# Pinned scans and logarithms, a new order at the end of the first tile's attention, and leaky factors on GpSimd

## The chip, the cores and the metric

One core of a Trainium2 chip runs the whole program. The metric is the device time of one execution in microseconds (us); less is better. The engines are named TensorE (PE, with its weight loads PEld), VectorE (DVE), ScalarE (ACT), GpSimd (POOL) and SyncE (SP, which issues most DMAs). Each engine has a queue of its own and does its instructions in the order in which they stand there; semaphores make one engine wait for another.

## What is computed

A gated linear attention over 4 batches, 8 heads, 768 tokens and head size 48, then a layer with a leaky activation whose slope alpha is given per column, then a gated layer. Cut to what matters:

```
for t in range(S):                       # q, k, v, alpha: (4, 8, 768, 48)
    state = alpha[:, :, t, :, None] * state + einsum('bhd,bhe->bhde', k[:, :, t], v[:, :, t])
    y[:, :, t] = einsum('bhd,bhde->bhe', q[:, :, t], state)
x = y.transpose(0, 2, 1, 3).reshape(B * S, H * D)          # 3072 x 384
h = x @ w_in                                               # 384 x 2048
x = (maximum(h, 0) + moe_alpha * minimum(h, 0)) @ w_out    # 2048 x 384
out = (((x @ w1) * (x @ w2)) @ w3) @ w_out2                # 384 x 1024, 1024 x 1024, 1024 x 384
```

The weights come as 64-bit words and are put together on the chip. Results have to keep float32 accuracy, so each factor of a large product is kept as an upper and a lower half (hi, lo), and three matmuls (hi by hi, lo by hi, hi by lo) take the place of one.

## The kernel before

**Attention.** The recurrence is done in 24 chunks of 128 tokens, n = 0 to 23, six to a batch. For each chunk `prep(n)` takes the running product of alpha over the chunk with a scan on VectorE (line 221, in place in one of two buffers, al), forms qt = q times that product (line 228), lets ScalarE take logarithm and exponential (r, lines 235 and 236) and forms kn from k and r in three VectorE steps (lines 237 to 239). GpSimd copies the last column (pend, line 232) and sets the first column of the buffer to zero (line 225). `scores(n)` multiplies qt and kn on TensorE (scp, line 244) and masks the result on VectorE (sc, line 279); `kT(n)` transposes kn (kTp, line 263; ScalarE copies it to kT). `chunk(n)` does the state matmuls (Up or uy), the update of the state on VectorE (`advance`: sst, lines 300 to 304), the output (`yout`: uy and yp) and then the scores of the next chunk. The outputs go by DMA into x, whose halves `xsplit` makes (hi on ScalarE, lo on VectorE, line 363).

**The two layers.** Four chunks make a tile T of 512 tokens, six tiles in all. A step (T, f) with f = 0 to 15 is `G1`, nine matmuls into h (line 407), and the activation: u on ScalarE (line 419), g on VectorE (line 421), gs hi on ScalarE (line 426), gs lo on VectorE (line 427); and `G2` two steps later, nine matmuls into three accumulator banks acc (lines 435 to 438). At f = 15 ScalarE copies the accumulators out (x1e), which frees their banks; uy, scp and kTp of the next tile's chunks use the banks of the same set. The factors sgn and salpha that u, g and gs take are computed from moe_alpha once, at the start. After tile 5 the gated layer follows from about 430 us on (ab, cs); the change does not touch it.

**What sets the order.** At the start a list of small functions, `first`, is run through: the attention of tile 0, with a few warm-up matmuls (wu) on zeros between them, so that TensorE is not idle. Then a sequence of steps mixes tile 0 with tile 1 (14 steps later) and goes through tiles 2 to 5 one after the other. After each `G1` and each `G2` the function `attend` runs some of the next tile's attention units, in the order that `attn_units` gives: chunk(n), kT(n + 1), prep(n + 2). In tile 0, and at every second step of tiles 2 to 4, a weight block is put together (`convert`: top on ScalarE, line 142; y on VectorE, line 149; for the first 16 blocks w hi on ScalarE and w lo on VectorE, line 154; the others go back to memory by DMA, line 182). The order of SyncE's DMAs is as written. On the other engines a scheduler may move an instruction ahead of ones written earlier where its inputs are ready; `keep_in_program_order` pins an instruction behind the one written before it on its engine. Before, pinned are u and g of tiles 2 to 5, the scan of chunk 4, and the y of some blocks.

Of the kernel before, what the change touches and what calls it, by code (L numbers as in the profile page):

```python
# [15 lines left out]
AF = mybir.ActivationFunctionType  # L16
AX = mybir.AxisListType
ALU = mybir.AluOpType
# [14 lines left out]
SPT = TA // CH  # L33
NTA = NT // TA
NF = DFF // 128
# [6 lines left out]
EARLY = 2  # L42
# [22 lines left out]
def fused_kernel(ctx, tc, qk, al, vv, wf, ws, m_alpha, ident, maskn, out):  # L65
# [3 lines left out]
    def f32(ap):  # L69
        return ap.bitcast(F32)  # L70

    def copy(out, in_):
        act.activation(out=out, in_=in_, func=AF.Copy)  # L73
# [93 lines left out]
    def convert(i, last=False):  # L167
        t = raw.pop(i)
        n = t.shape[1]
        if i == 0 or i >= NF:  # L170
            upper(top, t, i >= NF)
        y = cp.tile([128, n], I32, tag="y", name="y", bufs=1)
        ins = assemble(y, top, t)
        if last or i >= NF:
            tc.keep_in_program_order(ins)
        if i + 1 < NF:
            upper(top, raw[i + 1])
        if i < NF:
            split(wt[i][:, :, 0], wt[i][:, :, 1], f32(y).rearrange("p (o c) -> p o c", o=2), dve)
        else:  # L180
            c = (i - NF) * BLK
            later(1, lambda: sp.dma_start(out=ws_d[:, c:c + n], in_=f32(y)))
# [29 lines left out]
        v = st["v", n] = ap2.tile([128, H, DP], F32, tag="v", name="v", bufs=3)  # L212
        sp.dma_start(out=v, in_=vv[b, c])

    def prep(n, last=False):
        if n >= NSTEP:
            return
        t = st.pop(("qk", n))
        P = albuf[n % 2]
        flatP = P.rearrange("p a t -> p (a t)")  # L220
        scan = dve.tensor_tensor_scan(out=flatP, data0=flatP, data1=scan1.rearrange("p a t -> p (a t)"),  # L221
                                      initial=0.0, op0=ALU.mult, op1=ALU.max)
        if last:
            tc.keep_in_program_order(scan)
        pool.memset(P[:, :, 0:1], 0.0)
        Pv = P[:, :, 1:]
        qt = ap2.tile([128, NP, CH], F32, tag="qt", name="qt")
        dve.tensor_tensor(out=qt, in0=t[:, 0], in1=Pv, op=ALU.mult)
        r = ap2.tile([128, NP, CH], F32, tag="r", name="r", bufs=1)
        kn = ap2.tile([128, NP, CH], F32, tag="kn", name="kn")  # L230
        pend = ap2.tile([128, NP, 1], F32, tag="pend", name="pend")
        pool.tensor_copy(out=pend, in_=P[:, :, CH:])
        st["pend", n], st["qt", n], st["kn", n] = pend, qt, kn

        act.activation(out=r, in_=Pv, func=AF.Ln)
        act.activation(out=r, in_=r, func=AF.Exp, scale=-1.0)
        dve.tensor_tensor(out=kn, in0=t[:, 1], in1=r, op=ALU.mult)
        dve.tensor_tensor(out=r, in0=Pv, in1=r, op=ALU.mult)
        dve.scalar_tensor_tensor(out=kn, in0=r, scalar=2.0, in1=kn, op0=ALU.subtract, op1=ALU.mult)
# [44 lines left out]
    def state(n, w, ps):  # L284
        if ends(n):
            return
        t, v = st.pop(("kT", n)), st["v", n]
        for p, hh, r in pairs:
            mm(ps[r, p], t[:, p, r], v[:, 2 * p + hh], start=True, stop=True)

# [13 lines left out]
            dve.tensor_tensor(out=new, in0=new, in1=pend, op=ALU.mult)  # L304

    def yout(n, w, shared):
        qt, v = st.pop(("qt", n)), st.pop(("v", n))
        sc = [st.pop(("sc", n, hh)) for hh in range(2)]
        alone = n % NC_B == 0
        ps = [shared[:, 1] if n >= SPT else bank([128, NP // 2, CH], "yp", w), pab.tile([128, NP // 2, CH], F32, tag="h", name="yp")]  # L310
        half = [slice(64 * a, 64 * a + DP) for a in range(2)]
        for hh in range(2):
            for i in range(NP // 2):
                for a in range(2):
                    p = 2 * i + a
                    mm(ps[hh][half[a], i], v[:, 2 * p + hh], sc[hh][:, p], start=i == 0, stop=alone and i == NP // 2 - 1,
                       skip_group_check=True)
        if not alone:
            for i in range(NP // 2):
                for hh, a in ((0, 0), (1, 1), (0, 1), (1, 0)):  # L320
                    mm(ps[hh][half[a], i], sst[n % 2][half[hh], 2 * i + a], qt[half[hh], 2 * i + a], start=False,
                       stop=i == NP // 2 - 1, skip_group_check=True)
        T, c = divmod(n, SPT)
        if c == 0:
            new_x(T)
        single = n in (2, 3)
        if single:
            y = gp.tile([128, NP, CH], F32, tag="x1", name="yT1", bufs=KD)
            for hh in range(2):
                copy(y[:, 2 * hh:2 * hh + 2], ps[hh])  # L330
        else:
            if c % 2 == 0:
                st["yT"] = ap2.tile([128, KD, NP // 2, 2, CH], F32, tag="yT", name="yT", bufs=1)
            y = st["yT"]
            if n < SPT or ends(n):
                copy(y[:, 1, :, c % 2], ps[0])
            else:
                copy(y[:, :2, :, c % 2], shared)
                advance(n, y[:, 0, :, c % 2].rearrange("q i (a e) -> q i a e", a=2))
            copy(y[:, 2, :, c % 2], ps[1])  # L340
            if c % 2 == 0:
                return
            y = y[:, 1:].rearrange("p h i c t -> p (h i) (c t)")
        x = f32(xt[T][:, 1, :, (c if single else c - 1) * CH:(c + 1) * CH])

        def place():
            q = (sp, act) if n == SPT - 1 else (sp, sp)
            for hh in range(2):
                q[hh].dma_start(out=x[hh * D:(hh + 1) * D], in_=y[64 * hh:64 * hh + D, :KD])
            for i, (k, to, hh, e, n_) in enumerate(PIECES):  # L350
                q[i % 2].dma_start(out=x[to:to + n_, k], in_=y[64 * hh + e:64 * hh + e + n_, KD])

        later(1 if n < SPT or c == SPT - 1 else 4, place)
# [3 lines left out]
    def new_x(T):  # L357
        xt[T] = xp.tile([128, 2, KD, TA], F32R, tag="x", name="x")

    def xsplit(T, c, n):  # L360
        hi, lo = (xt[T][:, a, :, c * CH:(c + n) * CH] for a in range(2))
        copy(hi, f32(lo))
        dve.tensor_tensor(out=lo, in0=f32(lo), in1=f32(hi), op=ALU.subtract)

    def chunk(n, w, more=True):
        if n > 3:
            load_v(n + 2)
        untie()
        if n < SPT:
            ps = bank([128, NP, DP], "Up", w)  # L370
            state(n, w, ps)
            advance(n, ps)
            yout(n, w, None)
        else:
            ps = bank([128, 2, NP // 2, CH], "uy", w)
            state(n, w, ps[:, 0].rearrange("q i (a e) -> q (i a) e", a=2))
            yout(n, w, ps)
        if more:
            scores(n + 1, w)
        if n < 3:  # L380
            load_v(n + 3)
# [30 lines left out]
    def G1(T, f):  # L412
        x, w = xt[T], r_in[f]
        ps = pab.tile([128, TA], F32, tag="h", name="h")
        mm3(ps, [(w[:, i, k], x[:, 0, k]) for k in range(KD) for i in range(2)]
            + [(w[:, 0, k], x[:, 1, k]) for k in range(KD)], True, True)
        sg, sa = sgn[:, f:f + 1], salpha[:, f:f + 1]
        u = gp.tile([128, TA], F32, tag="m", name="u", bufs=1)
        both = [act.activation(out=u, in_=ps, func=AF.Identity, scale=sg)]  # L419
        gt = gp.tile([128, TA], F32, tag="g", name="g")  # L420
        both += [dve.scalar_tensor_tensor(out=gt, in0=ps, scalar=sa, in1=u, op0=ALU.mult, op1=ALU.max)]  # L421
        if T > 1:
            for ins in both:
                tc.keep_in_program_order(ins)
        s = g_t[T, f] = gp.tile([128, 2, TA], F32R, tag="gs", name="gs", bufs=3)
        act.activation(out=s[:, 0], in_=gt, func=AF.Identity, scale=sg)  # L426
        dve.scalar_tensor_tensor(out=s[:, 1], in0=gt, scalar=sg, in1=f32(s[:, 0]), op0=ALU.mult, op1=ALU.subtract)  # L427
# [17 lines left out]
    with tc.manual_schedule(engines={mybir.EngineType.SP}):  # L445
# [18 lines left out]
        def warm_up(n):  # L464
            ps = pab.tile([128, 512], F32, tag="h", name="wu")
            for _ in range(n):
# [6 lines left out]
        fetch(1)  # L473
        prep(1)
        load(3)
        dve.tensor_scalar(out=sgn, in0=alpha, scalar1=1.0, scalar2=-2.0, op0=ALU.is_gt, op1=ALU.mult)
        dve.tensor_scalar(out=sgn, in0=sgn, scalar1=1.0, scalar2=None, op0=ALU.add)
        dve.tensor_tensor(out=salpha, in0=alpha, in1=sgn, op=ALU.mult)
        first = [lambda: scores(0, 0), lambda: kT(0, 0), lambda: chunk(0, 0), lambda: (kT(1, 0), fetch(EARLY)), lambda: prep(2),
                 lambda: (load(4), chunk(1, 0)), lambda: kT(2, 0), lambda: prep(3),  # L480
                 lambda: chunk(2, 0), lambda: kT(3, 0), lambda: conv_next(True), lambda: xsplit(0, 0, 2),
                 lambda: chunk(3, 0, False), lambda: (warm_up(REST), conv_next(True), load(5)), lambda: (prep(4, True), load(6)),
                 lambda: xsplit(0, 2, 2)]
        for u in first:
            u()
            warm_up(WARM)
# [335 lines left out]
```

## Time and profile before

| | us |
|---|---|
| median of 3 runs | 847.43 |
| lowest, highest | 844.17, 847.84 |
| the profiled execution | 846.02 |
| its span in the trace | 844.2 |
| TensorE busy | 824.3 (98%) |
| VectorE busy | 458.3 (54%) |
| ScalarE busy | 355.3 (42%) |
| GpSimd busy | 10.3 (1%) |

The span runs from the first to the last instruction in the trace; what lies around it is 1.8 us. Busy shares are means over the whole span, and the start, the stretch with attention and the rest differ. The idle time that stands in brackets behind a row, with its releaser, is the time in which that engine had nothing to do ahead of that row.

### The profile page before, as it was taken

Reading aid. Unit: us, or ns where it says so; the run is one execution under the profiler, and the core shown is the slowest. Engines: PE = TensorE matmul, PEld = TensorE weight load, DVE = VectorE, ACT = ScalarE, POOL = GpSimd, SP = SyncE. Lnnn points to the kernel's source line nnn. Section 1 sums busy time; section 2 is a strip of 40 time slices with the busy share of each in tenths; the row PEclk is TensorE's granted clock in tenths of the full one; section 3 lists DMA queues with packets and bytes.
Section 4 is the critical chain, followed back from the end, with each engine's and each line's share of the span. In section 5 each row is a group of like instructions: output and inputs, shape, how many; then the busy total and the mean of one; then the engine's idle time right before and its main releaser. Section 6 shows DMA issues by size and latency. Waiting matters only on the chain.

```text
span 844.2 us, 12696 instructions
## 1 busy us (share of the span) xinstructions
PE 824.3 (98%) x5160; PEld 673.1 (80%) x5160; DVE 458.3 (54%) x643; ACT 355.3 (42%) x562; POOL 10.3 (1%) x53
## 2 busy tenths in 40 slices
PE   8989999999999999999999999999999999999996
PEld 4567888888887788878888889988888888888885
DVE  7799966774766576765345634652434425322221
ACT  4568764534544554554335634522223232222222
POOL 0000000000000000000000000000000000000000
PEclk9999999999999999999999999999999999999999
DMA  8647555330774377354104207320402203010101
GB/s 314 212 168 245 197 176 183 118 110 10 225 236 146 119 231 256 131 165 168 48 3 159 78 1 255 119 75 1 150 0 75 75 31 119 1 38 0 38 1 41
DMA packets 49106, 99.60 MB, mean 118 GB/s; under 512 B 4880, under 2 KB 25488, under 8 KB 49040
## 3 DMA queue, kind: packets, MB, share of 16 engines
q1 hardware_dynamic: 48800, 98.62, 34.6%
q8 instruction: 42, 0.69, 0.3%
q14 instruction: 24, 0.20, 0.1%
q10 hardware_dynamic: 240, 0.10, 0.0%
HBM read 75.63 MB, written 18.35 MB: 111 GB/s over the span
## 4 chain that ended last, share of the span: by engine, by line
PE 83%; DMA 2%; DVE 1%; ACT 1%; issue 0%; SPq 0%; DVEq 0%; ACTq 0%
PE ab L407 23%; PE h L407 20%; PE acc L407 12%; PE acc L435 6%; PE acc L438 6%; PE acc L436 6%; PE w L407 4%; PE uy L244 3%; DMA al<-in_al_dram 2%; PE scp L244 2%; PE yp L244 1%; PE kTp L263 1%; DVE al L221 0%; DVE y L149 0%; ACT u L419 0%
## 5 line engine op out<-in xcount | busy, mean ns | idle before, releaser
L407 PE MATMUL h<-x,w 128*128 128x512 f32 x864 | 214.3, 392 | 3.2 <-ACT w L73 1.4
L407 PE MATMUL ab<-x,w 128*128 128x512 f32 x864 | 203.6, 389 | 0.0
L407 PEld LDWEIGHTS h<-x,w 128*128 128x128 f32 x864 | 160.9, 188 | 39.8 <-DVE g L421 2.6
L407 PEld LDWEIGHTS ab<-x,w 128*128 128x128 f32 x864 | 162.1, 188 | 33.6
L435 PE MATMUL acc<-gs,w 128*128 128x512 f32 x288 | 114.7, 398 | 0.0
L614 DVE TENSOR_TENSOR c<-ab,a 128x512 f32<-128x512 f32 x48 | 33.1, 690 | 147.3 <-PE ab L407 147.3
L436 PE MATMUL acc<-gs,w 128*128 128x512 f32 x288 | 112.3, 390 | 0.0
L421 DVE SCALAR_TENSOR_TENSOR g<-h,salpha,u 128x512 f32<-128x512 f32 x96 | 71.8, 748 | 69.2 <-ACT u L419 69.1
L407 PE MATMUL acc<-cs,w 128*128 128x512 f32 x432 | 105.8, 389 | 0.0
L426 ACT ACTIVATE gs<-g,sgn 128x512 fp32r<-128x512 f32 x96 | 69.3, 722 | 75.5 <-DVE g L421 75.4
L419 ACT ACTIVATE u<-h,sgn 128x512 f32<-128x512 f32 x96 | 65.4, 681 | 82.5 <-PE h L407 82.4
L427 DVE SCALAR_TENSOR_TENSOR gs<-g,sgn,gs 128x512 fp32r<-128x512 f32 x96 | 71.9, 749 | 42.7 <-ACT gs L426 42.6
L407 PEld LDWEIGHTS acc<-cs,w 128*128 128x128 f32 x432 | 81.0, 188 | 17.2 <-DVE cs L617 0.4
L438 PE MATMUL acc<-gs,w 128*128 128x512 f32 x288 | 80.9, 389 | 0.0
L73 ACT ACTIVATE a<-ab 128x512 f32<-128x512 f32 x48 | 28.7, 597 | 111.9 <-PE ab L407 111.9
L73 ACT ACTIVATE cs<-c 128x512 fp32r<-128x512 f32 x48 | 30.2, 630 | 91.5 <-DVE c L614 91.5
L435 PEld LDWEIGHTS acc<-gs,w 128*128 128x128 f32 x288 | 54.1, 188 | 12.6 <-issue 1.2
L438 PEld LDWEIGHTS acc<-gs,w 128*128 128x128 f32 x288 | 54.1, 188 | 11.5
L436 PEld LDWEIGHTS acc<-gs,w 128*128 128x128 f32 x288 | 54.1, 188 | 10.5
L617 DVE TENSOR_TENSOR cs<-c,cs 128x512 fp32r<-128x512 f32 x48 | 33.2, 691 | 30.8 <-ACT cs L73 30.8
L142 ACT ACTIVATE top<-raw 128x768 f16<-128x768 bf16 (+1 forms) x39 | 41.8, 1071 | 16.9 <-DVE y L149 12.0
L221 DVE TENSOR_TENSOR_SCAN al<-al,scan 128x516 f32<-128x516 f32 x24 | 29.4, 1230 | 25.2 <-DMA al<-in_al_dram 25.2
(73 smaller groups left out, 673.8 us busy)
## 6 DMA issues: line engine op xcount, KB each, us to landing
raw<-in_ws_dram SPq DMA_DIRECT2D x22, 767.8 KB, 5.2
qk<-in_qk_dram SPq DMA_DIRECT2D x24, 512.0 KB, 5.9
raw<-in_wf_dram SPq DMA_DIRECT2D x16, 767.8 KB, 5.9
ws_d<-y SPq DMA_DIRECT2D x22, 384.0 KB, 2.6
al<-in_al_dram SPq DMA_DIRECT2D x24, 256.0 KB, 4.9
v<-in_vv_dram SPq DMA_DIRECT2D x24, 256.0 KB, 5.9
alx<-in_al_dram SPq DMA_DIRECT2D x8, 768.0 KB, 4.6
x_d<-x1e SPq DMA_DIRECT2D x18, 256.0 KB, 4.3
```

The costliest lines, as they stand in the source:

```text
L73: act.activation(out=out, in_=in_, func=AF.Copy)
L142: ins = act.activation(out=z[:, :n].bitcast(F16).rearrange("p (n c) -> p n c", c=2)[:, :, 1], in_=t.bitcast(BF16)[:, :, 2], func=AF.Copy)
L244: ins = pe.matmul(*a, **k)
L407: pe.matmul(ps, w, x, start=first and i == 0, stop=last and i == n - 1)
L419: both = [act.activation(out=u, in_=ps, func=AF.Identity, scale=sg)]
L421: both += [dve.scalar_tensor_tensor(out=gt, in0=ps, scalar=sa, in1=u, op0=ALU.mult, op1=ALU.max)]
L426: act.activation(out=s[:, 0], in_=gt, func=AF.Identity, scale=sg)
L427: dve.scalar_tensor_tensor(out=s[:, 1], in0=gt, scalar=sg, in1=f32(s[:, 0]), op0=ALU.mult, op1=ALU.subtract)
L435: pe.matmul(acc[T][m], r_out[f][:, 0, c], s[:, 0], start=f == 0, stop=False)
L436: pe.matmul(acc[T][m], r_out[f][:, 1, c], s[:, 0], start=False, stop=False)
L438: pe.matmul(acc[T][m], r_out[f][:, 0, c], s[:, 1], start=False, stop=f == NF - 1)
L617: dve.tensor_tensor(out=s[:, 1], in0=c, in1=f32(s[:, 0]), op=ALU.subtract)
```

## The change

It has six parts. (1) The scan and the logarithm of the preparations of chunks 9 to 23 are pinned behind the instruction written before them on their engine. (2) u and g are pinned from tile 1 on, where it was tile 2. (3) In `first`, the second weight conversion, load(5), the long warm-up and the second split of x are written inside prep(4), between its scan and its logarithm, instead of before and after prep(4); scan, logarithm and that split are pinned. (4) In chunk 3 the output is written ahead of the state matmuls and the update. (5) sgn and salpha are computed on GpSimd instead of VectorE; ahead of them the compiled program has one more row of GpSimd that loads a library. (6) The top half of weight block 2 is written at the conversion of block 2 itself, no more at that of block 1.

```
 def prep(n, last=False, between=None):
...
+        if last or n > 2 * SPT:
+            tc.keep_in_program_order(scan)
         if last:
-            tc.keep_in_program_order(scan)
+            between()
...
-        act.activation(out=r, in_=Pv, func=AF.Ln)
+        ln = act.activation(out=r, in_=Pv, func=AF.Ln)
+        if last or n > 2 * SPT:
+            tc.keep_in_program_order(ln)
         act.activation(out=r, in_=r, func=AF.Exp, scale=-1.0)
...
 def convert(i, last=False):
-        if i == 0 or i >= NF:
+        if i in (0, EARLY) or i >= NF:
             upper(top, t, i >= NF)
...
-        if i + 1 < NF:
+        if i + 1 < NF and i + 1 != EARLY:
             upper(top, raw[i + 1])
...
 def xsplit(T, c, n, last=False):
-        copy(hi, f32(lo))
-        dve.tensor_tensor(out=lo, in0=f32(lo), in1=f32(hi), op=ALU.subtract)
+        both = [act.activation(out=hi, in_=f32(lo), func=AF.Copy),
+                dve.tensor_tensor(out=lo, in0=f32(lo), in1=f32(hi), op=ALU.subtract)]
+        if last:
+            for ins in both:
+                tc.keep_in_program_order(ins)
...
 def chunk(n, w, more=True):
         if n < SPT:
+            if n == SPT - 1:
+                yout(n, w, None)
             ps = bank([128, NP, DP], "Up", w)
             state(n, w, ps)
             advance(n, ps)
-            yout(n, w, None)
+            if n < SPT - 1:
+                yout(n, w, None)
...
 def G1(T, f):
-        if T > 1:
+        if T > 0:
             for ins in both:
                 tc.keep_in_program_order(ins)
...
-        dve.tensor_scalar(out=sgn, in0=alpha, scalar1=1.0, scalar2=-2.0, op0=ALU.is_gt, op1=ALU.mult)
-        dve.tensor_scalar(out=sgn, in0=sgn, scalar1=1.0, scalar2=None, op0=ALU.add)
-        dve.tensor_tensor(out=salpha, in0=alpha, in1=sgn, op=ALU.mult)
+        pool.tensor_scalar(out=sgn, in0=alpha, scalar1=1.0, scalar2=-2.0, op0=ALU.is_gt, op1=ALU.mult)
+        pool.tensor_scalar(out=sgn, in0=sgn, scalar1=1.0, scalar2=None, op0=ALU.add)
+        pool.tensor_tensor(out=salpha, in0=alpha, in1=sgn, op=ALU.mult)
...
-                 lambda: chunk(3, 0, False), lambda: (warm_up(REST), conv_next(True), load(5)), lambda: (prep(4, True), load(6)),
-                 lambda: xsplit(0, 2, 2)]
+                 lambda: chunk(3, 0, False),
+                 lambda: prep(4, True, lambda: (conv_next(True), load(5), warm_up(REST), xsplit(0, 2, 2, True))),
+                 lambda: load(6)]
```

What the pins do to the order shows at three places. The first is VectorE in tiles 1 and 2, around the scan of chunk 14 (al_109 holds the even chunks, al_110 the odd ones). Before, it stands among the steps at the end of tile 1, right behind a kn of chunk 13:

```order
L279 TENSOR_TENSOR sc<-scp,msk 128x512 x2
L237 TENSOR_TENSOR kn<-qk,r 128x512
L221 SCALAR_TENSOR_TENSOR al_109<-al_109,scan_111 128x516
L238 TENSOR_TENSOR r<-al_110,r 128x512
L421 SCALAR_TENSOR_TENSOR g<-h,salpha,u 128x512
L239 SCALAR_TENSOR_TENSOR kn<-r,kn 128x512
```

After, it stands in tile 2, behind gs lo of that tile's third step, and qt, kn, r, kn follow it at once:

```order
L437 SCALAR_TENSOR_TENSOR gs<-g,sgn,gs 128x512
L431 SCALAR_TENSOR_TENSOR g<-h,salpha,u 128x512
L437 SCALAR_TENSOR_TENSOR gs<-g,sgn,gs 128x512
L221 SCALAR_TENSOR_TENSOR al_109<-al_109,scan_111 128x516
L230 TENSOR_TENSOR qt<-qk,al_109 128x512
L241 TENSOR_TENSOR kn<-qk,r 128x512
L242 TENSOR_TENSOR r<-al_109,r 128x512
L243 SCALAR_TENSOR_TENSOR kn<-r,kn 128x512
L306 TENSOR_TENSOR sst_112<-sst_113,yT 128x256
L149 SCALAR_TENSOR_TENSOR y<-raw,top 128x768
L431 SCALAR_TENSOR_TENSOR g<-h,salpha,u 128x512
```

So the scan went some ten steps back, from tile 1 to the last place ahead of its use. The second place is TensorE at that use, the scores of chunk 14, in the fourth step of tile 2. Before, they follow the output matmuls of chunk 13:

```order
L244 MATMUL uy<-qt,sst_113 64x128
L244 MATMUL yp<-qt,sst_113 64x128
L244 MATMUL scp<-qt,kn 64x128 x16
L435 MATMUL acc_2339<-gs,w_82 128x512
L436 MATMUL acc_2339<-gs,w_82 128x512
L435 MATMUL acc_2340<-gs,w_82 128x512
L436 MATMUL acc_2340<-gs,w_82 128x512
```

After, four accumulating matmuls of the next G2 have come ahead of them:

```order
L248 MATMUL uy<-qt,sst_113 64x128
L248 MATMUL yp<-qt,sst_113 64x128
L445 MATMUL acc_2336<-gs,w_82 128x512
L446 MATMUL acc_2336<-gs,w_82 128x512
L445 MATMUL acc_2337<-gs,w_82 128x512
L446 MATMUL acc_2337<-gs,w_82 128x512
L248 MATMUL scp<-qt,kn 64x128 x16
```

The third place is ScalarE at the end of tile 2, where the copies x1e free the accumulators. Before, the logarithm and the exponential of chunk 19 (the two rows r) stand between gs hi and these copies:

```order
L419 ACTIVATE u<-h,sgn 128x512
L426 ACTIVATE gs<-g,sgn 128x512
L235 ACTIVATE r<-al_110 128x512
L236 ACTIVATE r<-r 128x512
L73 ACTIVATE x1e<-acc_2339 128x512
L73 ACTIVATE x1e<-acc_2340 128x512
L73 ACTIVATE x1e<-acc_2341 128x512
```

After, the copies follow gs hi directly:

```order
L429 ACTIVATE u<-h,sgn 128x512
L436 ACTIVATE gs<-g,sgn 128x512
L73 ACTIVATE x1e<-acc_2336 128x512
L73 ACTIVATE x1e<-acc_2337 128x512
L73 ACTIVATE x1e<-acc_2338 128x512
L73 ACTIVATE yT<-uy 128x4x128
```

The two rows of chunk 19 now come five steps later, in tile 3.

## Rows read from the trace of the kernel before

**Rows 1.** The page, first part: TensorE (PE), its weight loads and the other engines, busy us, share of the span, count.

```profile
PE 824.3 (98%) x5160; PEld 673.1 (80%) x5160; DVE 458.3 (54%) x643; ACT 355.3 (42%) x562; POOL 10.3 (1%) x53
```

**Rows 2.** The table of two stretches: start and end, length, busy us of PE, PEld, DVE, ACT and POOL with their counts, granted clock, DMA share, GB/s.

```profile
50.00:60.00 10.00, 8.51 (x64) 6.26 (x62) 10.00 (x15) 6.23 (x10) 1.21 (x4) 1.00 0.71 248
400.00:700.00 300.00, 300.00 (x1394) 253.77 (x1393) 131.21 (x174) 106.90 (x175) 0.00 (x0) 1.00 0.24 78
```

**Rows 3.** The list of waits, those of TensorE: us in total, times, longest.

```profile
PE uy L244 <- ACT x1e L73: 2.4, 2, 1.4
PE Up L244 <- ACT kT L73: 1.9, 3, 1.2
PE scp L244 <- DVE kn L239: 1.7, 2, 1.4
PE h L407 <- ACT w L73: 1.4, 1, 1.4
```

**Rows 4.** The timeline at the end of tile 2 (start, length, engine, line, operation), and the scores of chunk 19.

```profile
285.79 1.23 DVE L221 TENSOR_TENSOR_SCAN al<-al,scan 128x516 f32<-128x516 f32 x1 [1.27 <-DMA al<-in_al_dram]
286.94 0.73 DVE L427 SCALAR_TENSOR_TENSOR gs<-g,sgn,gs 128x512 fp32r<-128x512 f32 x1
287.06 0.63 ACT L235 ACTIVATE r<-al 128x512 f32<-128x512 f32 x1 [1.78 <-DVE al L221]
...
287.72 0.63 ACT L236 ACTIVATE r<-r 128x512 f32<-128x512 f32 x1
288.25 1.55 ACT L73 ACTIVATE x1e<-acc 128x512 f32<-128x512 f32 x3
288.88 0.69 PE L244 MATMUL uy<-v,kT 128*64 128x64 f32 x16 [1.41 <-ACT x1e L73]
...
316.72 1.10 PE L244 MATMUL scp<-qt,kn 48*64 48x128 f32 x32
```

**Rows 5.** The timeline in tile 2 at 255 to 260 us.

```profile
255.76 1.23 DVE L221 TENSOR_TENSOR_SCAN al<-al,scan 128x516 f32<-128x516 f32 x1 [4.55 <-DMA al<-in_al_dram]
...
259.74 2.35 PE L407 MATMUL h<-x,w 128*128 128x512 f32 x9 [1.01 <-DVE g L421]
```

**Rows 6.** The timeline of one step of tile 2: h has ended at the first row, and the next h begins at the last.

```profile
278.70 0.39 PE L435 MATMUL acc<-gs,w 128*128 128x512 f32 x1
...
278.96 0.69 ACT L419 ACTIVATE u<-h,sgn 128x512 f32<-128x512 f32 x1 [0.88 <-PE h L407]
...
279.68 0.75 DVE L421 SCALAR_TENSOR_TENSOR g<-h,salpha,u 128x512 f32<-128x512 f32 x1 [0.61 <-ACT u L419]
...
280.47 0.72 ACT L426 ACTIVATE gs<-g,sgn 128x512 fp32r<-128x512 f32 x1 [0.82 <-DVE g L421]
...
280.74 2.20 PE L407 MATMUL h<-x,w 128*128 128x512 f32 x9
281.23 0.75 DVE L427 SCALAR_TENSOR_TENSOR gs<-g,sgn,gs 128x512 fp32r<-128x512 f32 x1 [0.79 <-ACT gs L426]
```

**Rows 7.** The timeline of a preparation that nothing else delays, that of chunk 0, from its exponential on; and one update of the state.

```profile
5.93 0.63 ACT L236 ACTIVATE r<-r 128x512 f32<-128x512 f32 x1
...
6.59 0.69 DVE L237 TENSOR_TENSOR kn<-qk,r 128x512 f32<-128x512 f32 x1 [0.39 <-ACT r L236]
7.32 0.69 DVE L238 TENSOR_TENSOR r<-al,r 128x512 f32<-128x512 f32 x1
8.04 0.69 DVE L239 SCALAR_TENSOR_TENSOR kn<-r,kn 128x512 f32<-128x512 f32 x1
...
261.74 0.42 DVE L302 TENSOR_TENSOR sst<-sst,yT 128x256 f32<-128x256 f32 x1
```

**Rows 8.** The timeline of TensorE at the end of the h ahead of the scores of chunk 14 and at these scores; between them the last kn of chunk 15, and behind them that chunk's scores.

```profile
213.84 0.39 PE L435 MATMUL acc<-gs,w 128*128 128x512 f32 x1
...
213.96 0.69 DVE L239 SCALAR_TENSOR_TENSOR kn<-r,kn 128x512 f32<-128x512 f32 x1
...
219.54 1.05 PE L244 MATMUL scp<-qt,kn 48*64 48x128 f32 x32
...
235.43 1.05 PE L244 MATMUL scp<-qt,kn 48*64 48x128 f32 x32
```

**Rows 9.** The timeline of TensorE in one chunk: the first state matmul and the scores.

```profile
253.43 0.69 PE L244 MATMUL uy<-v,kT 128*64 128x64 f32 x16
...
255.40 1.06 PE L244 MATMUL scp<-qt,kn 48*64 48x128 f32 x32
```

**Rows 10.** The timeline around 58 to 60 us: top of weight block 5, w hi of block 4 and the h that takes it.

```profile
58.20 1.07 ACT L142 ACTIVATE top<-raw 128x768 f16<-128x768 bf16 x1 [1.18 <-DMA raw<-in_wf_dram]
...
59.14 0.81 ACT L73 ACTIVATE w<-y 128x768 fp32r<-128x768 f32 x1
...
60.01 0.49 PE L407 MATMUL h<-x,w 128*128 128x512 f32 x1 [1.36 <-ACT w L73]
```

**Rows 11.** The timeline: the first of the three factor operations on VectorE, GpSimd's memset behind the scan of chunk 2, SyncE's load of chunk 4; and from the page's list of DMA issues (KB each, median us to landing) the loads of alpha.

```profile
14.58 0.17 DVE L476 TENSOR_SCALAR sgn<-alpha 128x16 f32<-128x16 f32 x1
16.43 0.10 POOL L225 MEMSET al<- 128x4 f32 x1 [6.26 <-DVE al L221]
19.55 0.55 SPq L204 DMA_DIRECT2D al<-in_al_dram  x1
al<-in_al_dram SPq DMA_DIRECT2D x24, 256.0 KB, 4.9
```

More of the change, by code (lines that the diff above doesn't have):

```diff
@@ L213, in load_v, with prep @@
         sp.dma_start(out=v, in_=vv[b, c])
-    def prep(n, last=False):
+    def prep(n, last=False, between=None):
         if n >= NSTEP:
@@ L286, in state @@
             return
-        t, v = st.pop(("kT", n)), st["v", n]
+        t, v = st.pop(("kT", n)), st.pop(("v", n)) if n == SPT - 1 else st["v", n]
         for p, hh, r in pairs:
@@ L306, in yout @@
     def yout(n, w, shared):
-        qt, v = st.pop(("qt", n)), st.pop(("v", n))
+        qt, v = st.pop(("qt", n)), st["v", n] if n == SPT - 1 else st.pop(("v", n))
         sc = [st.pop(("sc", n, hh)) for hh in range(2)]
@@ L358, in new_x, with xsplit @@
         xt[T] = xp.tile([128, 2, KD, TA], F32R, tag="x", name="x")
-    def xsplit(T, c, n):
+    def xsplit(T, c, n, last=False):
         hi, lo = (xt[T][:, a, :, c * CH:(c + n) * CH] for a in range(2))
-        copy(hi, f32(lo))
-        dve.tensor_tensor(out=lo, in0=f32(lo), in1=f32(hi), op=ALU.subtract)
+        both = [act.activation(out=hi, in_=f32(lo), func=AF.Copy),
[3 more added lines that the diff above has]
+                tc.keep_in_program_order(ins)
     def chunk(n, w, more=True):
```

## The prediction

> **What bounds the kernel now.** I read the page first: TensorE is busy for 824.3 us of a span of 844.2 [rows 1], so only what makes TensorE wait, or lets it wait less, can move the time. The profiled execution took 846.02 us; the sum below is made against that, and it lies 1.4 us under the median of the runs shown (847.43). Next the table by stretches, which says where TensorE is not full [rows 2]: from 400 to 700 us it has no gap at all, while from 50 to 60 us it has 8.51 of 10 and VectorE has 10.00 of 10. There is so little else to win: two kinds of places, the first 100 us and the stretch from 100 to 400 us, in which the attention of the later tiles is mixed in. Then the list of waits of TensorE [rows 3], whose entries I looked up in order of time. Two are at tile ends: the next tile's first state matmuls (uy) need accumulator banks that the copies x1e free, and ScalarE does the logarithm and the exponential of a preparation before those copies, because that preparation's scan on VectorE had stood waiting for its DMA [rows 4]. The scan there is that of chunk 19, whose scores run at 316.72 [rows 4], 31 us later: no hurry at all, yet its two ScalarE steps stand ahead of x1e. One wait has the same root in the middle of a tile: a scan at 255.76 that waited 4.55 us for its DMA, then a logarithm and an exponential ahead of u, and h started 1.01 late [rows 5].
>
> **The pins on scan and logarithm (chunks 9 to 23).** Before, the scheduler places a scan wherever it finds room, well ahead of its scores: the last kn of chunk 15 is at 213.96 and its scores start at 235.43 [rows 8]. After, the scan stands directly behind gs lo of the step ahead of which it is written, and the logarithm behind gs hi; everything of the preparation follows from there. So what I must ask is how long the chain is from the end of a step's h to the scores, and how much TensorE has to do meanwhile.
>
> The chain, counted from the end of h, which is the start of the row behind it: u begins at +0.26, g at +0.98, gs hi at +1.77, gs lo at +2.53 [rows 6]. The scan begins when gs lo's 0.75 us are over less an overlap of 0.08 (a row behind a scan of 1.23 starts 1.15 after it [rows 4]): +3.20. Scan to logarithm is 1.27, logarithm to exponential 0.66 [rows 4], exponential to kn 0.66, kn to r 0.73, r to the last kn 0.72, and that takes 0.69 [rows 7]. Together +7.93.
>
> TensorE's work in that time, from the order after: for the scores of chunk 14 it has seven accumulating matmuls of 0.227 (nine take 2.04 [rows 6]), nine of the next h (taken as 2.04 too), the state and output matmuls (1.97 [rows 9]), and four more accumulating matmuls that now stand ahead of the scores (0.91): 6.51. The wait is 7.93 - 6.51 = 1.4. The trace gives nearly the same without adding up: that h ended at 213.84 and the scores stood at 219.54 [rows 8]; 213.84 + 7.93 is 2.23 later, and the four matmuls fill 0.91 of it: 1.3.
>
> In the same way: chunks 9 and 10 have 7.0 us of work against 7.93 and two state updates (0.42 each [rows 7]), which half fit into the gaps of the chain, so 8.4: 1.4 each. Chunk 11 has one matmul more: 1.2. Chunk 12 has 7.85, but u stands between logarithm and exponential and gs lo in the chain (0.6 and 0.67), 9.2: 1.3. Chunk 15 has 7.7 against 9.2 (the lower half of x and one update lie in the chain): 1.5. Chunk 18: 6.9, 1.0. Chunk 19: 7.4 against 8.3, 0.9. Chunk 22 is as 14: 1.4. Chunk 23: 6.8 against 8.0, 1.2. Chunks 13, 16, 17, 20 and 21 have 10 us or a tile end in between: none. The ten make 12.7 us. I leave 0.3 either way on each, for rows that overlap differently: 9.7 to 15.7. What is queued behind the pinned scan on VectorE (qt, kn, the next g) and behind the logarithm on ScalarE (top, the next u) has two steps of time before G2 wants it, so it costs nothing beyond this; if that cover were gone at two places (chunks 15 and 19, where y stands there too), 0.4 each.
>
> **What the pins give back.** Behind tile ends ScalarE now does gs hi and then the three x1e copies; the logarithms of chunks 19 and 23 come later. That takes away 2.4 us [rows 3]. What is late next there is the last accumulating matmul itself, which TensorE has just done, so nothing. The wait of 1.01 [rows 5] goes too, since scan 17 is now behind gs lo of a later step. Together -3.4 us, bounds -2.4 to -3.4.
>
> **The first 100 us.** The new order writes the second conversion, load 5, the warm-up and the second split of x between scan 4 and its logarithm, and pins the split. ScalarE then reaches w of block 4 ahead of the top half of block 5, whose DMA it had waited for: the 1.36 us wait at 60.01 should go [rows 10]. Against it: the upper half of x stands behind top of block 2, so h of the first step starts some 0.5 to 1.0 later; top of block 4 is ahead of the copy of kT, so the state matmuls of chunk 4 wait up to 1.0 (one top is 1.07 [rows 10]); u and g of the second tile are pinned, which ties them behind a raw block's landing at two steps. VectorE is full there [rows 2] and gets back only the three factor operations. I take -0.5, and bound it by -3 and +3, since every one of these is of a size of one row of that engine. Output before state in chunk 3 moves 2 us of TensorE work in a stretch that warm-up matmuls fill: nothing. SyncE's order is the same row for row.
>
> **The factors on GpSimd.** VectorE loses three rows of 0.17 that stand in a row without idle time [rows 11]: -0.5 at most, included above. GpSimd gains three small operations and ahead of the first a row that loads its library. No row of the trace shows what that takes. GpSimd is idle for 6.26 us ahead of the memset at 16.43 [rows 11], and behind that the next to wait is SyncE's load of chunk 4 at 19.55, which needs the copy of the end values that GpSimd makes right behind that memset, another 2.8 or so: some 9 us are free. A load of 256 KB takes 4.9 us from issue to landing [rows 11], and by that nearest row the load is hidden: 0. The upper end is open, beyond 9 us it costs one for one.
> The Trainium skill (GPSIMD Engine Reference, 2.1 Instruction dispatch) says that the first call to freshly loaded code pays some 6 us that no instruction in a profile shows. No run here shows it so far; by it the sum is the same.
>
> **The sum.** 846.0 + 12.7 - 3.4 - 0.5 = 854.8. Against the median it would be 856.2; I say 855.0. With the bounds of the terms: 846.0 + 9.7 - 3.4 - 3 = 849.3 to 846.0 + 15.7 - 2.4 + 3 = 862.3.
>
> **The rivals.** (a) Faster: the chain does not end last. If it is shorter than TensorE's work (6.5 to 7.9 us), because the engines hand over faster here than in the rows I took, all of the 12.7 goes and only what is given back remains: 846.0 - 3.4 - 0.5 = 842.1. It decides from a chain of 6.5 us instead of 7.93, a fifth shorter. For it speaks that the trace has two waits of scores for kn in all [rows 3], so the old order was nowhere near the point; against it that every link is a dependency, and that the two orders differ in just this. Chance 0.13. (b) No change: the chain costs its 12.7, or 10 at its lower bound, but the first 100 us give more than I took. The waits for kT, kn and w that the list has there come to 5.0 [rows 3]; if all go and the chain costs its least, 846.0 + 9.7 - 3.4 - 5 = 847.3. For it speaks that VectorE is the bound there and is spared rows. Chance 0.17. (c) Much slower: GpSimd's library load takes 20 us, so 11 past the cover, and the loads and the first tile stand behind it: 855 + 11 = 866. Chance 0.05. That the pins do not do what they say I exclude, since the order of the instructions after shows every scan behind its gs lo. What is left, 0.65, is the forecast.
>
> **How the numbers follow.** Some 0.5%, 4.2 us, is what a measurement of this kernel can tell from no change: 843.2 and 851.7 are the limits. Slower by more: the forecast but its lowest part (0.62), and (c): 0.67. Faster: (a) but for its part within the limit, and a little of (b): 0.14. Within: 0.19. The range from 845 to 861 leaves out (a), some 0.12 of it, and (c) with the upper tail, 0.08.
>
> **What would show it.** Right: the list of waits of TensorE after has scores waiting for kn some ten times between 130 and 410 us, 0.9 to 1.5 each, and none for x1e; 13 us less of TensorE's busy share in that stretch. The row of the scan stands 3.2 us behind the end of an h. GpSimd's three rows lie before 20 us and VectorE waits for none of them. Wrong: waits for kn that are missing or under 0.5 (a); no waits for kT, kn and w left in the first 100 us, beside waits for scores of 1.0 or less (b); a gap of GpSimd of over 9 us ahead of its factors (c).

## The result and the profile after

The changed kernel takes 858.28 us (median of 4 runs, 856.53 to 860.29) beside 847.24 for the kernel before: ratio 1.0126, 95% interval 1.0102 to 1.015. It is 11 us slower, where the sum of the prediction had 8.8, and the time lies in the range. The profiled execution took 857.45 us with a span of 855.6, 11.4 more than before in both. The page's first part shows that TensorE is busy for 2 us more, and idle for 29 us of the span, where it was 20 [rows 1]:

```profile
PE 826.3 (97%) x5158; PEld 672.1 (79%) x5158; DVE 462.2 (54%) x640; ACT 357.5 (42%) x562; POOL 17.9 (2%) x56
```

The list of waits of TensorE after, in us in total, times, and longest:

```profile
PE scp L248 <- DVE kn L243: 13.5, 15, 1.6
PE h L417 <- DVE g L431: 2.3, 2, 1.7
...
PE Up L248 <- ACT kT L73: 1.7, 2, 1.3
PE h L417 <- ACT x L366: 1.0, 1, 1.0
```

The waits of scores for kn were 1.7 [rows 3] and are 13.5; those for x1e have left the list, and so has that of h for w. The timeline of TensorE shows where the scores wait from 130 us on (start, length, and in brackets the idle time ahead):

```profile
148.44 1.10 PE L248 MATMUL scp<-qt,kn 48*64 48x128 f32 x32 [1.04 <-DVE kn L243]
...
161.97 1.10 PE L248 MATMUL scp<-qt,kn 48*64 48x128 f32 x32 [1.32 <-DVE kn L243]
...
175.21 1.10 PE L248 MATMUL scp<-qt,kn 48*64 48x128 f32 x32 [0.81 <-DVE kn L243]
...
188.51 1.10 PE L248 MATMUL scp<-qt,kn 48*64 48x128 f32 x32 [0.82 <-DVE kn L243]
...
228.20 1.10 PE L248 MATMUL scp<-qt,kn 48*64 48x128 f32 x32 [1.07 <-DVE kn L243]
...
246.24 1.10 PE L248 MATMUL scp<-qt,kn 48*64 48x128 f32 x32 [1.00 <-DVE kn L243]
...
311.14 1.10 PE L248 MATMUL scp<-qt,kn 48*64 48x128 f32 x32 [0.79 <-DVE kn L243]
...
327.43 1.10 PE L248 MATMUL scp<-qt,kn 48*64 48x128 f32 x32 [0.51 <-DVE kn L243]
...
393.25 1.10 PE L248 MATMUL scp<-qt,kn 48*64 48x128 f32 x32 [1.07 <-DVE kn L243]
...
410.21 1.10 PE L248 MATMUL scp<-qt,kn 48*64 48x128 f32 x32 [0.85 <-DVE kn L243]
```

These are chunks 9 to 12, 14, 15, 18, 19, 22 and 23, the ten of the prediction and no other from 130 us on (the other five of the 15 waits in the list lie in the first 65 us). One of them in full, chunk 14, whose rows before are [rows 8]: the timeline of all engines from the end of h (first row) to its scores.

```profile
220.13 0.39 PE L445 MATMUL acc<-gs,w 128*128 128x512 f32 x1
...
220.39 0.69 ACT L429 ACTIVATE u<-h,sgn 128x512 f32<-128x512 f32 x1 [0.27 <-PE h L417]
...
221.12 0.75 DVE L431 SCALAR_TENSOR_TENSOR g<-h,salpha,u 128x512 f32<-128x512 f32 x1 [0.20 <-ACT u L429]
...
222.66 0.75 DVE L437 SCALAR_TENSOR_TENSOR gs<-g,sgn,gs 128x512 fp32r<-128x512 f32 x1 [0.79 <-ACT gs L436]
223.33 1.23 DVE L221 TENSOR_TENSOR_SCAN al<-al,scan 128x516 f32<-128x516 f32 x1
...
224.59 0.63 ACT L237 ACTIVATE r<-al 128x512 f32<-128x512 f32 x1 [1.96 <-DVE al L221]
...
225.25 0.63 ACT L240 ACTIVATE r<-r 128x512 f32<-128x512 f32 x1
...
225.91 0.69 DVE L241 TENSOR_TENSOR kn<-qk,r 128x512 f32<-128x512 f32 x1 [0.63 <-ACT r L240]
...
226.64 0.69 DVE L242 TENSOR_TENSOR r<-al,r 128x512 f32<-128x512 f32 x1
...
226.74 0.39 PE L446 MATMUL acc<-gs,w 128*128 128x512 f32 x1
...
227.37 0.69 DVE L243 SCALAR_TENSOR_TENSOR kn<-r,kn 128x512 f32<-128x512 f32 x1
...
228.20 1.10 PE L248 MATMUL scp<-qt,kn 48*64 48x128 f32 x32 [1.07 <-DVE kn L243]
```

The scan begins 3.20 after the end of h and the scores 8.07 after it, where 3.20 and 7.93 were worked out. At the end of tile 2, where [rows 4] had a wait of 1.41, the x1e copies now wait for TensorE and uy starts at once:

```profile
294.93 1.58 ACT L73 ACTIVATE x1e<-acc 128x512 f32<-128x512 f32 x3 [1.33 <-PE acc L448]
...
295.41 0.39 PE L446 MATMUL acc<-gs,w 128*128 128x512 f32 x1
295.73 0.69 PE L248 MATMUL uy<-v,kT 128*64 128x64 f32 x16
```

**By stage.** The scores of chunk 8 start at 134.31 (before 133.73), those of chunk 23 at 410.21 (398.00). So of the 11.4 us, 0.6 are lost in the first 130 us and 11.6 between these two; from there on 0.8 are given back. Most of that 0.8 was never lost: three accumulating matmuls of 0.227, 0.7 us in all, stand ahead of the scores of chunk 23 after, and behind them before, where the first acc of that step starts at 398.98 (timeline of TensorE after):

```profile
408.40 0.50 PE L445 MATMUL acc<-gs,w 128*128 128x512 f32 x1
408.74 0.39 PE L446 MATMUL acc<-gs,w 128*128 128x512 f32 x1
408.97 0.40 PE L445 MATMUL acc<-gs,w 128*128 128x512 f32 x1
```

### The profile page after: what moved, and what is told of

Read it like the earlier page. It is cut to its first block, busy times and chain, and to the rows that moved or that the text cites. A ratio compares the mean times of both kernels' runs of the same rounds, so it can differ in the third digit from the quotient of the medians.

```text
span 855.6 us, 12709 instructions
## 1 busy us (share of the span) xinstructions
PE 826.3 (97%) x5158; PEld 672.1 (79%) x5158; DVE 462.2 (54%) x640; ACT 357.5 (42%) x562; POOL 17.9 (2%) x56
## 4 chain that ended last, share of the span: by engine, by line
PE 73%; DVE 11%; ACT 6%; DMA 4%; issue 3%; SPq 1%; ACTq 0%; DVEq 0%
PE ab L417 23%; PE h L417 16%; PE acc L417 11%; PE acc L448 5%; PE acc L446 5%; PE acc L445 5%; PE w L417 4%; DMA raw<-in_wf_dram 2%; DVE al L221 2%; DVE g L431 2%; PE scp L248 2%; ACT u L429 1%; ACT gs L436 1%; DVE y L149 1%; DMA x<-yT 1%
## 5 line engine op out<-in xcount | busy, mean ns | idle before, releaser
L248 PE MATMUL scp<-qt,kn 48*64 48x128 f32 x768 | 26.3, 274 | 13.5 <-DVE kn L243 13.5
```

What stands on the lines that cost most here:

```text
L248: ins = pe.matmul(*a, **k)
```

## The experiments

Theory: the pinned scans put a chain behind gs lo that ends in the scores, and where TensorE has less to do than the chain is long, it waits. Rival one: the new order of the first tile, or GpSimd with its library, costs the time. Rival two: the pinned logarithm does it, by holding ScalarE. Rival three: each pin costs something wherever it stands. Beside each run's time stands the stretch from the scores of chunk 8 to those of chunk 23 in its profile, S; before it is 264.27 us, after 275.90. Where all ten of these chunks have their scans pinned in the written place (after, runs 2, 6, 7 and 8), S holds the 0.7 us of the three matmuls that only moved.

**1. No pins.** The kernel after, less the condition on n at both pins:

```diff
-        if last or n > 2 * SPT:
+        if last:
             tc.keep_in_program_order(scan)
...
-        if last or n > 2 * SPT:
+        if last:
             tc.keep_in_program_order(ln)
```

> The kernel after without the pins of scan and logarithm for chunks 9 to 23; all else stays. Theory (the pins put a chain behind a step's gs lo that ends in the scores): the ten waits for kn of 0.5 to 1.3 us go, the two waits for x1e and the one for g (3.4 us together) come back, the first 100 us stay as in the kernel after: 858.3 - 13.9 + 2.9, so 847 to 848. Rival one (the new order of the first tile or GpSimd's library costs the time): 857 or more.

Measured 846.44 us, ratio to before 1.0003 (0.9986 to 1.0021), S 263.61. No wait for kn is left from 130 us on, and the two waits for x1e are back, though not the one for g (timeline of TensorE):

```profile
288.32 0.69 PE L248 MATMUL uy<-v,kT 128*64 128x64 f32 x16 [1.63 <-ACT x1e L73]
...
368.55 0.69 PE L248 MATMUL uy<-v,kT 128*64 128x64 f32 x16 [1.34 <-ACT x1e L73]
```

All that is left of the change besides the pins is worth nothing that can be measured, either way. Rival one falls.

**2. The scan's pin alone.** The second of the two edits of run 1.

> The kernel after with the scans of chunks 9 to 23 pinned and their logarithms not. Theory: the logarithm follows its scan anyway, so the chain is as long as before this edit: 857 to 859, ten waits of the scores for kn. Rival two (the logarithm behind gs hi is what delays the chain and ScalarE's other work): the waits go, 845 to 848.

Measured 856.77, ratio 1.0116 (1.0093 to 1.0139), S 275.77: the whole loss, and just under the 857 that I gave as the least. Rival two falls as an explanation of it.

**3. The logarithm's pin alone.** The first of the two edits of run 1.

> The kernel after with the logarithms of chunks 9 to 23 pinned and their scans not. Theory: the scan is done early, and the chain begins with the logarithm behind gs hi at +2.5 us after the end of h: exponential, kn, r, kn end at +5.9, which TensorE's 5.6 to 7 us of work cover but for 0.3 at some chunks; the waits for x1e do not come back, since the logarithm of chunk 19 stays behind the copies: 844 to 846.5. Rival two: as the kernel after, 857 to 859.

Measured 849.96, ratio 1.0034 (1.0016 to 1.0051), S 267.23: over a quarter of the loss (3.6 of 12.3 us in S), where I expected next to nothing. The waits for x1e stay away, but six waits for kn remain in S, five of 0.26 to 0.69 and one of 1.51 (chunk 15). In the latter's chain the halves of x stand: the upper half on ScalarE between logarithm and exponential (240.11), and the lower half on VectorE ahead of kn, behind a wait for the upper:

```profile
239.71 0.75 DVE L437 SCALAR_TENSOR_TENSOR gs<-g,sgn,gs 128x512 fp32r<-128x512 f32 x1 [0.79 <-ACT gs L436]
240.97 0.96 DVE L367 TENSOR_TENSOR x<-x 128x768 fp32r<-128x768 f32 x1 [0.50 <-ACT x L366]
241.85 0.68 DVE L241 TENSOR_TENSOR kn<-qk,r 128x512 f32<-128x512 f32 x1
```

So the logarithm's pin has a price as well, by the same chain from a later link on.

**4. All pins, but the preparation earlier.** In the kernel after, for tiles 2 to 5:

```diff
             u += [lambda n=n, ahead=ahead: (ahead and load(n + 3), chunk(n, w, ahead)),
+                  *([lambda n=n: prep(n + 2)] if T > 1 else []),
                   lambda n=n, ahead=ahead: ahead and kT(n + 1, w)]
-            if T > 1 or n < n0 + SPT - 2:
+            if T == 1 and n < n0 + SPT - 2:
                 u += [lambda n=n: prep(n + 2)]
```

> The kernel after with all its pins, but prep(n + 2) is written ahead of kT(n + 1) instead of behind it in tiles 2 to 5, which moves every pinned scan some step (4 us of TensorE work) forward. Theory: 4 us are more than the 0.5 to 1.3 that were short at each of the ten chunks, so no wait of the scores for kn is left from 130 us on, and those for x1e stay away: 844 to 846. Rival (the pins cost by taking freedom from the scheduler at large, or by the switches between short and long matmuls, not by the length of this chain): 852 or more.

Measured 848.70, ratio 1.0023 (1.0009 to 1.0037), S 265.43. With every pin kept, 10.5 of the 12.3 us by which S is longer with the pins than without (263.61) are gone; 0.7 of these are the matmuls that moved. Of the ten waits, that of chunk 9 stays (1.03), whose preparation is written elsewhere and did not move, and one of 0.29; five of 0.15 to 0.48 for other things are new. The time is 2.7 us above the range that I gave and 3.3 under the rival's. The waits left in S come to 2.5 us, where run 1 has 3.0 at x1e, and still S is 1.8 longer than in run 1; that part is not in the list of waits.

**5 and 6. The pins where there is room, and where there is none.** The kernel after with both pins on five chunks, and on the other ten:

```diff
-        if last or n > 2 * SPT:
+        if last or n in (13, 16, 17, 20, 21):
```

```diff
-        if last or n > 2 * SPT:
+        if last or n in (9, 10, 11, 12, 14, 15, 18, 19, 22, 23):
```

> The kernel after with the pins of scan and logarithm on chunks 13, 16, 17, 20 and 21 alone: the five where TensorE has 10 us or a tile end between the scan and the scores. Theory (a pin costs what the chain is longer than TensorE's work there): no wait for kn from 130 us on, and since scan 17 and scan 21 are held back, the logarithms of chunks 19 and 23 come behind the x1e copies, so the 3.0 us of waits that the run without pins has there go too: 846.4 - 3.0, so 843 to 844.5. Rival (each pin costs some 1 us, wherever it stands): 846.4 + 5 x 1, so 850 or more.

> The kernel after with the pins on the other ten chunks alone (9 to 12, 14, 15, 18, 19, 22, 23). Theory: all ten waits of the scores stay, and those for x1e stay away since the logarithms of chunks 19 and 23 are still pinned: as the kernel after, 856.5 to 859. Rival (each pin costs the same): 846.4 + 10 x 0.9, the same, so this run tells the two apart only beside the run of the other five.

With room: 845.69, ratio 0.9981 (0.997 to 0.9993), S 263.30. Five pins cost nothing, so rival three falls; but the time is 1.2 us above the range that I gave. The waits for x1e are gone here too, but h waits for g twice in their place, 0.25 and 1.16, the latter since two preparations come close together on ScalarE. Without room: 861.02, ratio 1.0177 (1.0154 to 1.02), S 279.39, all ten waits, and 2 us above what I gave. Two of the waits are longer than in the kernel after, chunk 12 with 2.20 for 0.82 and chunk 19 with 1.96 for 0.51. VectorE in that run, around the chain of chunk 19, shows why:

```profile
322.20 1.23 DVE L221 TENSOR_TENSOR_SCAN al<-al,scan 128x516 f32<-128x516 f32 x1 [2.57 <-DMA al<-in_al_dram]
323.35 0.73 DVE L437 SCALAR_TENSOR_TENSOR gs<-g,sgn,gs 128x512 fp32r<-128x512 f32 x1
...
327.07 1.23 DVE L221 TENSOR_TENSOR_SCAN al<-al,scan 128x516 f32<-128x516 f32 x1
328.33 1.29 DVE L230 TENSOR_TENSOR qt<-qk,al 128x512 f32<-128x512 f32 x2
```

The free scan of chunk 20 (first row) moved ahead and held VectorE for 2.57 us for its DMA, with g and gs behind it; and its qt stands inside the chain of chunk 19 (two qt in the last row). Chunk 12 has the same (a free scan at 177.61 that waited 2.51, and a second qt in the chain). A longer chain makes a longer wait, as the theory has it. A part of the 2 us is something else: behind the wait of 2.20 the granted clock of TensorE was at the lower of its two levels (1.2 GHz for 2.4) for a while. The table by stretches has it at 0.87 from 190 to 192 us, at 0.78 from 194 to 196, and between them at 0.50 (busy us of PE, PEld, DVE, ACT and POOL with their counts, granted clock, DMA share, GB/s):

```profile
192.00:194.00 2.00, 2.00 (x9) 1.49 (x5) 1.98 (x4) 0.00 (x0) 0.00 (x0) 0.50 0.95 349
```

The shares that are missing come to 0.85 of a stretch of 2 us, so up to 1.7 us of S, by estimate.

**7. The pins on the kernel before.** All of the change left out but the pins:

```diff
-        if last:
+        if last or n > 2 * SPT:
             tc.keep_in_program_order(scan)
...
-        act.activation(out=r, in_=Pv, func=AF.Ln)
+        ln = act.activation(out=r, in_=Pv, func=AF.Ln)
+        if n > 2 * SPT:
+            tc.keep_in_program_order(ln)
```

> The kernel before with the pins of scan and logarithm for chunks 9 to 23 and nothing else of the change. Theory: the pins are the whole change in time, 856 to 859 beside 847. Rival one (the new order of the first tile or the factors on GpSimd take part of it, or only the two together lose): under 853.

Measured 857.45, ratio 1.0119 (1.01 to 1.0138), S 274.84. Without the rest of the change, the pins cost the whole of it.

**8. The factors on VectorE again.** In the kernel after, `pool.` becomes `dve.` in the three lines for sgn and salpha.

> The kernel after with sgn and salpha on VectorE again. Theory: three rows of 0.17 in a stretch of the start that is not bound by VectorE alone, and no library load that anything waits for: within 0.5 of the kernel after, 857 to 859. Rival (the library load on GpSimd costs several us): 854 or less.

Measured 858.38, ratio 1.0129 (1.0108 to 1.0149), S 274.92: as the kernel after.

**9 and 10. Towards a better version.** The kernel before with the logarithms of chunks 17, 19 and 23 pinned; and the kernel before with the five pins of run 5 on scan and logarithm.

```diff
+        if n in (17, 19, 23):
+            tc.keep_in_program_order(ln)
```

```diff
+        if last or n in (13, 16, 17, 20, 21):
             tc.keep_in_program_order(scan)
...
+        if n in (13, 16, 17, 20, 21):
+            tc.keep_in_program_order(ln)
```

> The kernel before with the logarithms of chunks 17, 19 and 23 pinned and nothing else: the three that stand ahead of x1e or u where TensorE then waits. Theory: the waits for x1e (1.41 and 1.02) and for g (1.01) go, and the chain from the pinned logarithm of chunks 19 and 23 (behind gs hi of a step, +5.9 us after the end of its h) is as long as TensorE's work there to within 0.4; so 846.8 - 3.4 + 0.5, 843 to 845. Rival (what is taken from these waits comes back as another wait, as the run with five pins showed in part): 845.5 to 847.

> The kernel before with scan and logarithm of chunks 13, 16, 17, 20 and 21 pinned and nothing else. Theory: as the same pins in the kernel after without the other ten (845.7), since the first 100 us make no difference: 845 to 846.5.

Run 9: 847.63, ratio 1.0009 (0.9992 to 1.0025), S 265.60: above both ranges, and as the rival has it. The three waits it aimed at are gone, and two others take their place (timeline of TensorE):

```profile
256.56 0.66 PE L246 MATMUL yp<-sc,v 128*64 128x128 f32 x8 [2.22 <-DVE g L423]
...
319.18 1.10 PE L246 MATMUL scp<-qt,kn 48*64 48x128 f32 x32 [1.35 <-DVE kn L241]
```

Ahead of the first, a scan still waited for its DMA (5.15 us, as in [rows 5]), now ahead of g itself. It is that of chunk 18, not of chunk 17 as my expectation had it (more below). Behind this wait of 2.22 the granted clock fell too (0.91, 0.50 and 0.74 in the three stretches of 2 us from 256 us on), again up to 1.7 us. Run 10: 845.14, ratio 0.9975 (0.9962 to 0.9988), S 263.52. It is the only edit of the kernel before that is faster than both kernels, by a quarter of a per cent.

## Why the prediction was right

**The chain.** Right in place, in mechanism and nearly in size. For chunk 14 it was 8.07 us for 7.93. All ten chunks wait that were named, and none of the five others. The sum was 12.7; the list of waits has 9.3 for them, but that is not all they cost. S grew by 11.6 although 3.4 of waits went and 0.55 came new (h for g at 366.67); 0.7 of it is work that only moved. So the ten chunks cost 11.6 + 3.4 - 0.55 - 0.7 = 13.8, or 1.4 each, inside the bounds of 9.7 to 15.7. Chunk 14 gives the same without the list: its scores stood 5.70 behind the end of h [rows 8], now they stand 8.07 behind it, and the four matmuls that came ahead of them fill 0.91, so 1.46 are lost where 1.3 to 1.4 was worked out.

The difference to the list is 0.45 at each, and the rows of chunk 14 show most of it. The last matmul ahead of the scores starts at 226.74, and matmuls of its kind follow one another after 0.227, so the true gap is 228.20 - 226.97 = 1.23 where the list has 1.07. And the four matmuls moved ahead of the scores make two changes between long and short matmuls more, 0.11 us each in the rows (an acc behind scores takes 0.34 to the next row, 229.24 to 229.58, and not 0.23). The sum had no term for these changes.

Two signs of the prediction came out smaller than it said. The waits are 0.51 to 1.32, five of the ten under the 0.9 that it gave as the least. And TensorE's idle time from 130 to 415 us rose from 3.4 to 10.1 us, so by 6.7 and not by 13 (first row before, second after):

```profile
130.00:415.00 285.00, 281.56 (x2226) 230.53 (x2225) 184.83 (x266) 141.11 (x223) 4.10 (x28) 1.00 0.46 154
130.00:415.00 285.00, 274.89 (x2177) 220.81 (x2176) 186.41 (x264) 139.27 (x218) 9.79 (x30) 1.00 0.47 152
```

**What the pins give back.** Right: -3.4 was said, and the waits for x1e and the one for g are gone; 0.55 came back elsewhere. One reading was wrong and did no harm: the scan at 255.76 [rows 5] is that of chunk 18, not of chunk 17, whose last kn ends at 248.3. Scan 18 is pinned as well and starts at 306.27 after, so the wait goes all the same. In run 9 logarithm 17, pinned, runs at 271.40 and logarithm 18 behind it at 274.89, while the scan of chunk 18 stayed where it was. That the -3.4 is a gain by itself is not shown: where a run took these waits away without the chain's loss (4, 5, 9 and 10), between a third and all of it came back as other waits (1.2, 1.4, 3.6 and 1.8 us).

**The first 100 us.** -0.5 was said, with 3 either way; the scores of chunk 8 start 0.6 later. The wait for w at 60.01 is gone as foretold, and in its place are 1.05 at the first h, 0.83 for kT, 1.63 of the scores of chunk 6 for kn (64.46) and 1.72 for g at 95.31; of these the prediction had named all but the one of chunk 6. A difference of 0.6 is small beside what this part varies by between executions (last section), and run 1 puts the sum at no difference that can be measured.

**GpSimd.** Right. After its copy at 9.99 us it waits 1.23 us for a DMA and does the first factor at once (timeline of GpSimd after):

```profile
9.99 0.67 POOL L234 COPY pend<-al 128x4 f32<-128x4 f32 x1
11.90 0.29 POOL L486 TENSOR_SCALAR sgn<-alpha 128x16 f32<-128x16 f32 x1 [1.23 <-DMA alpha<-in_m_alpha_dram]
15.94 0.10 POOL L227 MEMSET al<- 128x4 f32 x1 [3.75 <-DVE al L221]
```

The gap between the two operations is 11.90 - 10.66 = 1.24 us. The 6 us of the Trainium skill (GPSIMD Engine Reference, 2.1 Instruction dispatch) do not show here; the library row, wherever it takes its time, holds back nothing. Run 8 agrees. That GpSimd is busy for 7.6 us more after is not the library either: 7.1 of it are its copies pend, 593 ns each for 294 before, and 653 in run 8, which has no factors on GpSimd.

**The rivals.** (a), a chain shorter than TensorE's work, is refuted by the ten waits; (b) by run 1, since the first 100 us give nothing; (c) by the rows of GpSimd and run 8. The sum was 854.8 where the profiled execution took 857.45: the chain's term was 1.1 short (13.8 for 12.7), the first part 1.1 (0.6 for -0.5), a new wait brought 0.55, and 0.1 came back behind the scores of chunk 23; 2.65 in all.

## What to carry to other kernels

An instruction pinned to the place where it is written is as late as what is written ahead of it, so before pinning, add up the chain from there to its consumer and set it against the work that the busy engine has in that time: five pins with 10 us of work or a tile end in between cost nothing, ten with 6.5 to 7.9 us against a chain of 8 to 9 cost 14 us. The scheduler's early scans looked untidy, since they stood waiting for their DMA on VectorE, but what they cost (3.4 us) was a quarter of what the pinned order cost. To take a wait away at one place is worth little while the same engines are as tight a step later.

## What the runs showed of the hardware that I had not expected

The list of waits understates what this order costs TensorE: 9.3 us are listed for the ten chunks and 13.8 were lost, of which 0.16 at chunk 14 is the tail of the matmul ahead and 0.11 goes with each change between long and short matmuls, as worked out above.

Executions differ most where I had not looked. S lies between 274.84 and 275.90 in the four runs with all the pins in the written place on the scans (after, 2, 7 and 8), while the scores of chunk 8, ahead of it, start at 133.73 in the profile of before and at 137.81 in run 7, which is written the same up to there (its scan of chunk 9, now pinned, no longer runs ahead of them), and at 134.31 after and 138.68 in run 8, which differs only in the three factors. A part of these 4 us goes with the granted clock of TensorE. In the first 130 us it was 1.00 before and after, and 0.97 in runs 7 and 8 (before, run 7, after, run 8):

```profile
0.00:130.00 130.00, 120.67 (x1005) 88.69 (x1006) 110.35 (x160) 79.26 (x119) 6.21 (x25) 1.00 0.65 221
0.00:130.00 130.00, 119.66 (x987) 87.36 (x988) 106.24 (x153) 77.19 (x115) 6.18 (x23) 0.97 0.64 213
0.00:130.00 130.00, 117.72 (x1001) 87.79 (x1002) 107.28 (x152) 78.00 (x116) 8.15 (x26) 1.00 0.64 220
0.00:130.00 130.00, 116.75 (x982) 86.68 (x983) 105.55 (x153) 76.47 (x114) 7.83 (x23) 0.97 0.64 213
```

In stretches of 2 us it stands at 1.00 but for two falls to 0.50, the lower level, in each of the two runs (run 7 from 14 and from 78 us on, run 8 from 64 and from 98 us on). Each fall takes away 1.7 us of full clock, so by estimate up to 3.4 of the 4.1 and 4.4 us. How much of it reached the scores is not shown: run 10 has one fall in this part and starts them at 137.09, run 6 has one too and starts them at 134.34. Three of the four falls stand right behind a wait of TensorE (1.63 at 78.84 in run 7, 1.63 at 64.69 and 2.74 at 98.08 in run 8). But a wait of 1.63 at 64.46 in the profile of after had no fall behind it, so why the clock fell in one execution and not in another is open.
